# Another order of the products, output steps and side work of a convolution with a SwiGLU feed-forward

## The chip, the cores and the metric

The kernel runs on one core of a Trainium2 chip. The metric is the device time of one execution in microseconds (us). A measurement is the median of several executions; a profile is one more execution, taken by the hardware profiler. Engines are called by the profile's names: PE is TensorE (PEld its weight loads), DVE is VectorE, ACT is ScalarE, POOL is GpSimd, and SP is SyncE, whose queue issues nearly all DMAs (SPq).

## The reference

The input is x of 8 x 4096 tokens with 192 channels. A causal convolution over seven tokens with weights per head (eight heads of 24 channels, softmax over the seven taps) makes the tokens of a feed-forward network: RMS norm, two products with 192 x 1536 matrices, SiLU of one times the other, and a product with a 1536 x 192 matrix.

```python
w = np.exp(weight - weight.max(-1, keepdims=True)); w = w / (w.sum(-1, keepdims=True) + 1e-09)
out = np.einsum('hk,bskhg->bshg', w, x_unf)          # x_unf: 7 shifted copies of x, padded at the front
x = out.reshape(B * S, D)
xn = x / np.sqrt(np.mean(x * x, axis=-1, keepdims=True) + 1e-06) * rms_g
g = xn @ w_gate
val = xn @ w_val
return (g * (1.0 / (1.0 + np.exp(-g))) * val @ w_out).astype(np.float32)
```

## The kernel before

The 32768 tokens are cut into 32 *pairs* of 2 x 512 tokens (numbered 0 to 31). Pairs 0 and 1 run in their own way at the start, while the weights are converted and split into parts that go to DRAM (`wd`); pairs 2 to 31 are alike, and the change concerns them and the end of pair 1.

**Products of a pair (line 909).** The 1536 columns are handled in six groups j = 0 to 5, each with four cells a, b, c, d (two token halves times two column blocks). Each cell needs a gate and a value matrix product, which lie in the two halves of one *duo* of PSUM banks; there are four duos. A product is six matmuls, three parts of two, on 64 rows and 128 columns of the array. For j = 1 and 3 a cell is the sum of its products A, B, E. For j = 0, 2, 4, 5 a Strassen form with eleven products is used: P1, Q1, P2 go into a; P6, P7, Q3, P4 into b; P5, Q2, P3 into c; Q4 into d. Between them stand copies and sums in PSUM: f1 copies a to b (ACT, line 674) after P1 and before P6; f3 copies c to the scratch tile `tt` after P5 (ACT line 674, or DVE line 676); f4 makes c = b + tt (DVE, line 980) after P6 and before P7 and P3; f5 makes d = b + tt (line 980) after P7 and before P4, Q3 and Q4. So a.0, f4.5 and so on name a cell or an act and its group.

When a cell is complete, ga to gd take the SiLU (ACT, line 986) and ma to md multiply (DVE, line 993) into `ht`; both together give the duo back. A product that opens a cell (P1, P5, A) takes the duo that came free.

**Output steps (line 936).** Form and group, o1.0 to o7.5: 42 steps per pair, a Strassen form again, each of twelve matmuls on 128 rows and 32 columns of the array, into accumulators X, Z and Y, a duo each. The sums of halves h1 to h4 (DVE or POOL, line 963) prepare the operands of o5, o6, o7 and o3. After the o1 steps c1 copies X to Y; after o7, s7 copies Z, after o6, c2 copies X (ACT, line 674); at the end C22 and C21 add (DVE, line 1010), and the transposes T11, T12, T21, T22 (DVE, line 951) fill `o_sb`, from where st writes the output (line 1042) and which give X, Y, Z back.

**Work for later pairs.** ld loads rows of x (line 153) two pairs ahead; cv0 to cv6 are the taps of the convolution (ACT line 440, DVE line 444); sq, red, pow, bc, mul are the norm; pl stores the result to DRAM (line 1053); ft fetches it transposed (line 645) into `xb`. x1 to x4 are four sums of token halves (line 831); n, l, d split each of five operand groups 0 to 4 into three parts (n: ACT line 674; l: line 817; d: DVE line 819). Group 0 serves P1 and A, 1 serves P2, P4 and B, 2 the Q and E, 3 P5 and P6, 4 P7 and P3. The split weights come through a *ring* of ten slots; each use of a slot that is its last issues the next load (line 789). R, at the end of the first window, starts the ring.

**What sets the order.** Three strings written out by hand or by a planner. `LINE` is the order of products and steps in a pair. `ORDER` is one *window*: it interleaves the next n words of the line ("p4") with the acts; the first letter is the engine (V, A, G, S), a "+" means the next pair, a "-" the one before. It runs for windows 2 to 32. `FIRST` is window 1 (pair 1), in which W are pieces of the weight preparation. Every engine takes its instructions strictly in this order.

In before, the window begins with the last 15 steps of the pair before, then P1.0, and the 42 steps of a pair stand in one run.

Of the kernel before, what the change touches and what calls it, by code (L numbers as in the profile page):

```python
# [20 lines left out]
def kernel(  # L21
# [55 lines left out]
        "a5 b5 c5 d5",  # L77
    )
    ORDER = (
        "p4- Vd.3 Vl.3 Gh4.0- Gh4.2- p3- Vl.4 Vh4.1- Gl.1 Vd.4 Vh4.3- Vd.2 Vh4.5- Vcv1+ VC22-",  # L80
        "VT11- p8- Vcv2+ VT22- Vl.2 VC21- p1 Af1.0 VT12- VT21- p1 Af3.0 p1 Vcv3+ p1 Vf4.0 p2",
        "Vcv4+ p5 Agb.1 Vmb.1 Agc.0 Vf5.0 p1 Vmc.0 p1 Agd.0 Aga.0 p4 Sst0.0- Aga.1 Sst1.4-",
        "Sst0.1- Vcv5+ Vma.0 Vcv6+ Vma.1 Vmd.0 p1 Agb.0 p1 Asq+ p1 Vmb.0 Vred+ p1 Af1.2 p1",
        "Agc.3 Vmc.3 p4 Af3.2 Vf4.2 p2 Aga.2 Gpow+ p3 Vbc+ Vma.2 Vf5.2 Gmul+ p1 Spl.0+ Agc.2",
        "p2 Agd.3 Spl.1+ Sst1.2- Spl.2+ Agb.2 Vmc.2 Vmd.3 Spl.3+ Vmb.2 Vh1.0 Agd.2 p7 Agc.1",
        "Vmc.1 Vmd.2 Af1.4 p3 Agd.1 Vmd.1 Spl.4+ Spl.5+ Vf3.4 p2 Spl.6+ Vf4.4 Aga.4 Spl.7+ p2",
        "Vma.4 p2 Vf5.4 Agc.4 p3 Agb.3 Vmb.3 Vmc.4 p1 Agb.4 p2 Agd.4 Sft.0+ Sft.1+ Sft.2+",
        "Sst0.4- Vmb.4 Gh1.1 Gh1.2 Gh1.3 Sld.0++ Sft.3+ p1 Vmd.4 Af1.5 p1 Af3.5 Sld.1++",
        "Sld.2++ Sst1.0- p2 Aga.3 Vh3.2 Vf4.5 Vma.3 Sft.4+ Sld.3++ Sld.4++ Sld.5++ Sft.5+",
        "Sld.6++ Sst0.2- Sld.7++ Sst0.3- Sst1.1- Sst1.3- p3 Vf5.5 Aga.5 p4 Gh1.4 Gh3.1 Agc.5",  # L90
        "Gh3.4 p1 Vma.5 Gh3.0 Gh3.3 Vmc.5 An.0+ p1 Vx3+ Agd.5 Agb.5 Vl.0+ p5 Vmd.5 p2 Vmb.5",
        "Vh2.1 An.1+ Ac1 Vh1.5 Vx1+ p2 Gh2.0 Vh3.5 Vd.1+ Vx2+ Vh2.5 Vh2.2 Vh2.3 Vh2.4 p4",
        "Vh4.4 Vd.0+ Vx4+ p8 An.3+ An.4+ As7 Ac2 An.2+ Acv0++ p5",
    )
    FIRST = (
        "p1 Vcv5+ W p2 Vcv6+ p1 Aga.0 Vma.0 p2 Asq+ W W p1 Agb.0 W Vmb.0 W p1 Vred+ p2 Agc.0",
# [4 lines left out]
        "Vmc.2 p1 W p1 W W W p1 Agd.2 W p1 Vmd.2 W Vh1.2 p2 Vh3.2 Vh2.2 p1 Aga.3 W Vma.3 p1 W",  # L101
        "W W p1 W W p1 Agb.3 Sft.0+ Vmb.3 Sft.1+ p1 Sft.2+ p1 Sft.3+ W p1 Sft.4+ Agc.3 W W W",
        "Sft.5+ Vmc.3 p1 W W p2 Agd.3 p1 Vmd.3 Vh1.3 p1 W p1 W W Vh3.3 Vh2.3 W p1 Aga.4 W",
        "Vma.4 p3 Agb.4 W Vmb.4 p1 W p2 Agc.4 Vx3+ Vmc.4 p2 An.1+ p1 Agd.4 Vx1+ p1 Vmd.4",
        "Vd.1+ Vh1.4 p1 Vx2+ p1 Vh3.4 Vh2.4 Sld.0++ Vx4+ p1 Aga.5 Vma.5 An.3+ p2 An.2+ p1",
        "Agb.5 Vmb.5 p1 Sld.1++ p2 Gl.1+ Agc.5 Sld.2++ Vmc.5 p1 Vd.2+ p1 Vl.2+ Agd.5 p1 Vmd.5",
        "An.0+ Vl.0+ Vd.0+ An.4+ p1 Vh1.5 p1 Sld.3++ p1 Ac1 Sld.4++ Vh3.5 Vh2.5 p2 Sld.5++ p1",
        "Vh4.4 p1 Sld.6++ p1 R p2 Sld.7++ p6 As7 p1 Ac2 p4 Acv0++",
    )
    LINE = (  # L110
        "P1.0 P5.0 Ab.1 P6.0 Bb.1 Eb.1 P7.0 P3.0 Q2.0 P2.0 Q1.0 Q4.0 Aa.1 Ea.1 Ba.1 P4.0 Q3.0",
        "Ac.3 Ec.3 P1.2 Bc.3 P5.2 P6.2 Q1.2 P2.2 Ad.3 Ed.3 P7.2 Q2.2 P3.2 Bd.3 Q4.2 P4.2 Q3.2",
        "Ac.1 Ec.1 Bc.1 Ad.1 P1.4 Bd.1 Ed.1 P5.4 P6.4 Q1.4 Ab.3 P2.4 Eb.3 P7.4 Q2.4 P3.4 Bb.3",
        "Q3.4 P4.4 Q4.4 Aa.3 P1.5 Ea.3 P5.5 P6.5 Ba.3 Q1.5 P2.5 P7.5 Q2.5 P3.5 P4.5 Q3.5 Q4.5",
        "o1.0 o1.1 o7.0 o7.3 o1.2 o1.3 o1.5 o1.4 o7.2 o7.1 o2.4 o2.5 o6.0 o2.1 o6.3 o6.5 o2.2",
        "o7.5 o6.2 o6.4 o7.4 o6.1 o2.3 o4.0 o5.1 o5.5 o5.4 o5.0 o5.2 o5.3 o2.0 o4.5 o4.4 o4.3",
        "o3.1 o4.2 o4.1 o3.4 o3.3 o3.0 o3.5 o3.2",
    )

    cst = ctx.enter_context(tc.tile_pool(name="cst", bufs=1))  # L120
# [1176 lines left out]
```

## Time and profile before

| | |
|---|---|
| median of 3 executions | 2484.42 us (2483.5 to 2485.6) |
| profiled execution | 2486.79 us |
| its span | 2485.0 us |
| PE busy | 2464.4 us (99%) |
| DVE busy | 2051.4 us (83%) |
| ACT, POOL busy | 993.1 us (40%), 795.2 us (32%) |
| granted TensorE clock | 0.999 |

Busy time of an engine is the time in which one of its instructions runs; a matmul's end is modelled, so a waiting PE can be counted as busy, and starts of instructions tell more than busy shares. In the timelines a row is: start in us from the span's start, length, engine, line, operation, output <- inputs, shape, count, and in brackets the idle time before it with what ended it.

### The profile page before, as it was taken

What the parts mean: (1) busy time and instruction counts of PE and PEld (TensorE: products, weight loads), DVE (VectorE), ACT (ScalarE), POOL (GpSimd) and SP (SyncE); (2) the same over time, 40 slices, a digit from 0 to 9 for tenths busy, and PEclk for the clock granted to TensorE, in tenths of its full rate; (3) what the DMA queues carried; (4) which work ended last, traced back from release to release, by engine and by line L of the source; (5) the groups of instructions that cost most, each with busy time, mean ns of one, the idle gap of its engine ahead of it and who ended that gap; (6) DMA issues with size and microseconds to landing.
All of it is one profiled execution on the core that took longest, in us unless ns stands there. A gap on an engine that the chain in (4) does not pass through costs nothing.

```text
span 2485.0 us, 69316 instructions
## 1 busy us (share of the span) xinstructions
PE 2464.4 (99%) x29152; PEld 1923.9 (77%) x29152; DVE 2051.4 (83%) x2614; ACT 993.1 (40%) x1405; POOL 795.2 (32%) x566
## 2 busy tenths in 40 slices
PE   8999999999999999999999999999999999999998
PEld 5547778878787777788887778877788777888876
DVE  8688888888888888888888888888887888888864
ACT  6443334434344434344334343333344343444332
POOL 0541332323332323323323324233423233333222
PEclk9999999999999999999999999999999999999999
DMA  6364678666677666787667786666776666776653
GB/s 151 60 205 127 167 182 211 178 172 168 170 193 198 179 165 171 175 204 185 182 161 175 179 206 185 173 164 172 187 200 185 171 168 170 199 192 186 161 159 92
DMA packets 716392, 430.55 MB, mean 173 GB/s; under 512 B 510330, under 2 KB 702386, under 8 KB 716082
## 3 DMA queue, kind: packets, MB, share of 16 engines
q1 hardware_dynamic: 712336, 425.21, 66.6%
q8 instruction: 230, 3.77, 0.6%
q10 hardware_dynamic: 3746, 0.92, 0.2%
q14 instruction: 80, 0.66, 0.1%
HBM read 366.96 MB, written 58.98 MB: 171 GB/s over the span
## 4 chain that ended last, share of the span: by engine, by line
PE 94%; DVE 2%; DMA 1%; SPq 1%; issue 1%; POOL 0%; ACT 0%; DVEq 0%; POOLq 0%
PE ps L909 57%; PE ps L936 35%; PE ps L881 2%; DMA ht<-in_moe_w_gate_dram 0%; SPq L237 0%; DVE ht L1108 0%; DVE ht L963 0%; SPq L153 0%; DVE y L444 0%; DMA xb<-xd 0%; DMA x<-in_x_dram 0%; DMA hs<-in_moe_w_out_dram 0%; DVE part L344 0%; DMA ring<-wd 0%; POOL part L335 0%
## 5 line engine op out<-in xcount | busy, mean ns | idle before, releaser
L909 PE MATMUL ps<-part,ring 64*128 64x512 f32 x12240 | 1434.0, 390 | 2.6 <-DVE ps L980 0.4
L909 PEld LDWEIGHTS ps<-part,ring 64*128 64x128 f32 x12240 | 1174.3, 184 | 255.3 <-DVE ps L980 32.3
L986 ACT ACTIVATE tt<-ps 128x512 f32<-128x512 f32 x744 | 436.1, 599 | 714.4 <-PE ps L909 636.0
L993 DVE TENSOR_TENSOR ht<-ps,tt 128x512 f32<-128x512 f32 x744 | 495.5, 686 | 195.6 <-ACT tt L986 192.4
L936 PE MATMUL ps<-ht,wo_sb 128*32 128x384 f32 (+2 forms) x7272 | 471.6, 380 | 0.8 <-POOL wo_sb L336 0.8
L963 POOL TENSOR_TENSOR ht<-ht 128x512 f32<-128x512 f32 x182 | 279.0, 1563 | 568.7 <-PE ps L936 568.7
L936 PE MATMUL ps<-ht,x 128*32 128x256 f32 (+2 forms) x6696 | 429.1, 379 | 1.3 <-DVE ht L963 1.3
L936 PEld LDWEIGHTS ps<-ht,wo_sb 128*32 128x32 f32 x7272 | 332.4, 110 | 102.4 <-DVE tt L831 9.4
L980 DVE TENSOR_TENSOR ps<-ps,tt 128x1024 f32<-128x1024 f32 x240 | 295.6, 1232 | 97.8 <-ACT tt L674 55.6
L936 PEld LDWEIGHTS ps<-ht,x 128*32 128x32 f32 x6696 | 299.0, 110 | 87.5 <-DVE ht L963 2.0
L444 DVE SCALAR_TENSOR_TENSOR y<-xh,tp,y 128x1536 f32<-128x1536 f32 x186 | 338.9, 1822 | 2.5 <-ACT y L440 2.3
L674 ACT COPY ps<-ps 128x1024 f32<-128x1024 f32 (+1 forms) x151 | 134.0, 887 | 478.6 <-PE ps L909 367.9
L963 POOL TENSOR_TENSOR hs<-ht 128x512 f32<-128x512 f32 x120 | 165.5, 1390 | 405.2 <-DVE ht L993 405.2
L473 POOL TENSOR_SCALAR r<-r 128x8 f32<-128x8 f32 x31 | 6.1, 198 | 484.5 <-DVE r L468 484.4
L674 ACT COPY tt<-ps 128x1024 f32<-128x1024 f32 (+1 forms) x152 | 121.6, 800 | 68.7 <-PE ps L936 57.9
L963 DVE TENSOR_TENSOR ht<-ht 128x512 f32<-128x512 f32 x190 | 132.5, 698 | 9.7 <-PE ps L936 6.4
L936 PE MATMUL ps<-hs,x 128*32 128x128 f32 (+2 forms) x2232 | 130.1, 379 | 0.0
L936 PEld LDWEIGHTS ps<-hs,x 128*32 128x32 f32 x2232 | 94.0, 110 | 30.7
L674 ACT CAST part<-tt 128x1024 fp32r<-128x1024 f32 x60 | 62.9, 1049 | 136.8 <-DVE tt L831 136.8
L963 DVE TENSOR_TENSOR ht<-hs,ht 128x512 f32<-128x512 f32 x156 | 106.7, 729 | 1.2 <-PE ps L936 0.6
L819 DVE SCALAR_TENSOR_TENSOR part<-part,xb 128x1024 fp32r<-128x1024 f32 x87 | 105.9, 1218 | 0.0
L817 POOL TENSOR_TENSOR part<-xb,part 128x1024 fp32r<-128x1024 f32 x29 | 96.6, 3329 | 0.0
(131 smaller groups left out, 1436.5 us busy)
## 6 DMA issues: line engine op xcount, KB each, us to landing
ring<-wd SPq DMA_DIRECT2D x1440, 192.0 KB
xb<-xd SPq DMA_DIRECT2D x60, 512.0 KB
xd<-xh SPq DMA_DIRECT2D x240, 96.0 KB
xh<-in_x_dram SPq DMA_DIRECT2D x192, 105.0 KB
xb<-xd SPq DMA_DIRECT2D x60, 256.0 KB
out_dram<-o_sb SPq DMA_DIRECT2D x126, 96.0 KB
out_dram<-o_sb SPq DMA_DIRECT2D x62, 128.0 KB
wd<-part SPq DMA_DIRECT2D x5, 1152.0 KB
```

The costliest lines, as they stand in the source:

```text
L444: nc.vector.scalar_tensor_tensor(out=y, in0=xk, scalar=w, in1=y, op0=ALU.mult, op1=ALU.add)
L473: nc.gpsimd.tensor_scalar(out=r, in0=r, scalar1=s / D, scalar2=s * 1e-6, op0=ALU.mult, op1=ALU.add)
L674: nc.scalar.copy(out=dst, in_=src)
L817: e.tensor_tensor(out=split_of(g, 1).bitcast(F32R), in0=src, in1=high, op=ALU.subtract)
L819: nc.vector.scalar_tensor_tensor(out=split_of(g, 2).bitcast(F32R), in0=high, scalar=1.0 + SPLIT, in1=src, op0=ALU.mult, op1=ALU.subtract,)
L881: nc.tensor.matmul(out=self.both(j, c)[:, h, :], lhsT=wf[HALF[h], k, 2 * HOME[j] + f, :], rhs=rb[HALF[h], k, g, :], start=(k == 0), stop=( ...
L909: nc.tensor.matmul(out=self.both(j, c)[:, h, :], lhsT=left[HALF[h]], rhs=right[HALF[h]], start=(first and q == 0), stop=True, skip_group_c ...
L936: nc.tensor.matmul(out=self.acc(b)[i * Q : (i + 1) * Q, at : at + n], lhsT=left, rhs=cols, start=fresh, stop=True, skip_group_check=True, ...
L963: engine[eng].tensor_tensor(out=dst, in0=a, in1=b, op=op)
L980: nc.vector.tensor_tensor(out=self.both(j, c), in0=self.both(j, "b"), in1=s5, op=ALU.add)
L986: nc.scalar.activation(out=tt[:, t, :], in_=self.both(j, c)[:, 0, :], func=AF.Silu)
L993: nc.vector.tensor_tensor(out=self.hv(j, "abcd".index(c)), in0=self.both(j, c)[:, 1, :], in1=tt[:, t, :], op=ALU.mult,)
```

## The change

`ORDER`, `FIRST` and `LINE` are replaced by others; nothing else in the program changes. The multiset of products, steps and acts of a pair is the same, but:

- `LINE`: the 42 steps of a pair now stand in three places: five o1 steps after P7.5, then P4.5, Q3.5, Q4.5; then six steps; then the first product of the next pair, P1.0; then the other 31 steps. Inside the pair, groups are arranged anew: six products instead of three from P6.0 to P7.0, P3.5 ahead of P7.5, P5.4 ahead of P1.4.
- `ORDER`: a window begins with P1.0. With it, acts move over the window's edge: s7, c2, h2.4, h4.4 are done in the next window, and n.1 to n.4, d.1, x2 to x4 and cv0 stand at the head of the window of their pair.
- Engines: f3.4 moves from VectorE to ScalarE; x2, h1.0, h2.2, h3.2, h4.1 and l.4 from VectorE to GpSimd; h2.0, h3.1, h3.3, h4.0, h4.2 and l.1 from GpSimd to VectorE.
- `FIRST`: holds 83 words of pair 1's line instead of 99, so that pair 2's P1.0 comes ahead of 31 of pair 1's steps. All eight loads of pair 3's rows (Sld) stand behind R, where seven stood before it.

```diff
     ORDER = (
-        "p4- Vd.3 Vl.3 Gh4.0- Gh4.2- p3- Vl.4 Vh4.1- Gl.1 Vd.4 Vh4.3- Vd.2 Vh4.5- Vcv1+ VC22-",
-        "VT11- p8- Vcv2+ VT22- Vl.2 VC21- p1 Af1.0 VT12- VT21- p1 Af3.0 p1 Vcv3+ p1 Vf4.0 p2",
-        "Vcv4+ p5 Agb.1 Vmb.1 Agc.0 Vf5.0 p1 Vmc.0 p1 Agd.0 Aga.0 p4 Sst0.0- Aga.1 Sst1.4-",
...
+        "Gx2 p1 p6- An.3 An.1 p1- An.2 As7- Vh2.4- Vl.2 Vl.3 Vd.3 Vh4.0- p5- Ac2- Acv0+ p12-",
+        "Vx3 Vx4 Vd.1 Vd.2 Vl.1 p1- Vcv1+ Vh4.2- Vh4.3- Vh4.4- Vcv2+ VC22- Vh4.5- VT11- Vcv3+",
+        "VC21- Af1.0 An.4 p3- VT22- Gh4.1- Gl.4 p2- VT21- p1- VT12- p2 Af3.0 p5 Vd.4 Vf4.0",
+        "Vcv4+ Aga.0 Vma.0 p1 Agb.1 p2 Vmb.1 Vf5.0 p4 Vcv5+ p1 Agc.0 Vmc.0 p3 Aga.1 Agd.0",
+        "Agb.0 Vcv6+ Asq+ Vmd.0 p1 Vmb.0 Vma.1 Af1.2 p1 Vred+ p1 Agc.3 Af3.2 p3 Gpow+ Vmc.3",
...
+        "An.0+ p2 Gh1.4 Gh3.2 Gh3.4 Gh2.2 p2 Vh2.0 Vf5.5 Vmc.5 p3 Agb.5 Agd.5 Vd.0+ p1 Vx1+",
+        "Vl.0+ p2 Vmd.5 Vmb.5 Ac1 Vh2.1 Vh1.5 Vh2.3 Vh3.5 p3 Vh2.5",
     )
     FIRST = (
...
-        "An.0+ Vl.0+ Vd.0+ An.4+ p1 Vh1.5 p1 Sld.3++ p1 Ac1 Sld.4++ Vh3.5 Vh2.5 p2 Sld.5++ p1",
-        "Vh4.4 p1 Sld.6++ p1 R p2 Sld.7++ p6 As7 p1 Ac2 p4 Acv0++",
+        "Vd.2+ p1 Vl.1+ Agc.5 Vmc.5 p2 Agd.5 p1 Vmd.5 An.0+ Vd.0+ Vl.0+ p1 Ac1 Vh1.5 p2 Vh3.5",
+        "Vh2.5 p2 R Sld.0++ Sld.1++ Sld.2++ Sld.3++ Sld.4++ Sld.5++ Sld.6++ Sld.7++",
     )
     LINE = (
-        "P1.0 P5.0 Ab.1 P6.0 Bb.1 Eb.1 P7.0 P3.0 Q2.0 P2.0 Q1.0 Q4.0 Aa.1 Ea.1 Ba.1 P4.0 Q3.0",
...
-        "Q3.4 P4.4 Q4.4 Aa.3 P1.5 Ea.3 P5.5 P6.5 Ba.3 Q1.5 P2.5 P7.5 Q2.5 P3.5 P4.5 Q3.5 Q4.5",
+        "P1.0 P5.0 P6.0 Ab.1 P2.0 Eb.1 Q1.0 Bb.1 P7.0 Q2.0 P3.0 Aa.1 Ba.1 P4.0 Ea.1 Q4.0 Q3.0",
...
+        "P5.4 Ac.1 P1.4 Ec.1 Bc.1 P6.4 Q1.4 P2.4 Ad.1 Bd.1 Ed.1 Ab.3 Bb.3 P7.4 P3.4 Q2.4 Eb.3",
+        "P4.4 Q4.4 Q3.4 Aa.3 P1.5 Ea.3 P5.5 P6.5 Ba.3 Q1.5 P2.5 P3.5 Q2.5 P7.5 o1.0 o1.2 o1.4",
+        "o1.3 o1.5 P4.5 Q3.5 Q4.5 o7.0 o1.1 o7.1 o7.4 o7.3 o6.0 o6.1 o2.5 o6.5 o7.2 o2.0 o6.3",
...
     )
```

## The prediction

> **What bounds the kernel now.** I read the page first (its head, its busy times, its chain), then TensorE's timeline over one pair in the middle of the run, then the timeline of its weight loads over the same pair, and at last the start of the pipeline.
>
> The page of before:
>
> ```profile
> span 2485.0 us, 69316 instructions
> ...
> PE 2464.4 (99%) x29152; PEld 1923.9 (77%) x29152; DVE 2051.4 (83%) x2614; ACT 993.1 (40%) x1405; POOL 795.2 (32%) x566
> ...
> PE 94%; DVE 2%; DMA 1%; SPq 1%; issue 1%; POOL 0%; ACT 0%; DVEq 0%; POOLq 0%
> PE ps L909 57%; PE ps L936 35%; PE ps L881 2%; DMA ht<-in_moe_w_gate_dram 0%; SPq L237 0%; DVE ht L1108 0%; DVE ht L963 0%; SPq L153 0%; DVE y L444 0%; DMA xb<-xd 0%; DMA x<-in_x_dram 0%; DMA hs<-in_moe_w_out_dram 0%; DVE part L344 0%; DMA ring<-wd 0%; POOL part L335 0%
> ```
>
> TensorE is the chain: products (L909) and output steps (L936) are 92% of the span. But a stalled matmul counts as busy here, so waits must be read from starts. TensorE's timeline (start, length, engine, line, count), one pair:
>
> ```profile
> 1198.85 47.87 PE L909 MATMUL ps<-part,ring 64*128 64x512 f32 x408
> 1246.65 1.51 PE L936 MATMUL ps<-ht,wo_sb 128*32 128x384 f32 x24
> ...
> 1274.09 1.32 PE L909 MATMUL ps<-part,ring 64*128 64x512 f32 x8
> ```
>
> A pair takes 1274.09 - 1198.85 = 75.23 us: 68 products (408 matmuls) in 47.80, 42 steps in 27.44. Where nothing waits, products start 0.680 us apart (Q4.2 to P6.4, eighteen in a row), so 68 need 46.24. Steps start 0.645 to 0.650 apart; 42 x 0.650 = 27.30, and 0.137 is left at the end of the run. The product part is 47.80 - 46.24 = 1.56 too long. The weight loads of that part say where (in brackets: idle of the load path, and what ended it):
>
> ```profile
> 1198.85 0.53 PEld L909 LDWEIGHTS ps<-part,ring 64*128 64x128 f32 x6 [0.20 <-issue]
> 1199.67 3.30 PEld L909 LDWEIGHTS ps<-part,ring 64*128 64x128 f32 x30 [0.29 <-DVE o_sb L951]
> 1203.42 3.28 PEld L909 LDWEIGHTS ps<-part,ring 64*128 64x128 f32 x30 [0.45 <-DVE ps L980]
> 1207.14 24.42 PEld L909 LDWEIGHTS ps<-part,ring 64*128 64x128 f32 x216 [0.44 <-issue]
> 1231.79 7.36 PEld L909 LDWEIGHTS ps<-part,ring 64*128 64x128 f32 x66 [0.23 <-DVE ps L980]
> 1239.31 4.65 PEld L909 LDWEIGHTS ps<-part,ring 64*128 64x128 f32 x42 [0.15 <-ACT ps L674]
> 1244.35 1.93 PEld L909 LDWEIGHTS ps<-part,ring 64*128 64x128 f32 x18 [0.39 <-DVE ps L980]
> ```
>
> Normally a load runs 0.23 ahead of its matmul. Each bracket is a load that could not. By counts they are P5.0 (waits for the transpose T12), P7.0 (f4.0), Q4.0 (f5.0), P7.4 (f4.4), P6.5 (the copy f1.5), P4.5 (f5.5). From starts over 30 pairs, in medians, with the slow matmuls just behind: P5.0 0.20, P7.0 0.34, Q4.0 0.30, P7.4 0.11, P4.5 0.28, P6.5 0.05, and P6.2 0.07, whose load is late inside the long line. Together 1.35; the other 0.21 is the change of tiling, next. One law fits them: the cost is release + 0.13 us - due start (P6.2 released 0.06 early: 0.07; P7.4 0.02 early: 0.11; P7.0 0.19 late: 0.33).
>
> **Extra: four changes of tiling per pair.** Now each pair has one run of steps. After, it has three: five steps before P4.5, six before the next pair's P1.0, 31 behind it. Pair 1 already alternates, without waits at the joints:
>
> ```profile
> 182.82 0.86 PE L936 MATMUL ps<-ht,wo_sb 128*32 128x384 f32 x12
> 183.61 10.57 PE L881 MATMUL ps<-xb,part 64*128 64x512 f32 x48
> 194.11 1.51 PE L936 MATMUL ps<-ht,x 128*32 128x384 f32 x24
> ```
>
> A lone step takes 183.61 - 182.82 = 0.787, 0.137 over 0.650. The 48 matmuls between take 10.50 where 24 pairs of them at 0.429 need 10.30: 0.20 more. A round trip costs 0.337 there, and 0.347 by pair 15's own joints (0.106 into steps, 0.137 and 0.104 back). Two more round trips in each of 30 pairs: 60 x 0.347 = **+20.8 us**. These bounds are close; I take the row of the same kind of product.
>
> **Waits that go.** f4 starts 0.97 after its P6 starts (or f5 after P7), lasts 1.23 (group L980), and the load wants 0.05 + 0.13 more: 2.38 us, 3.5 products. P6.0 to P7.0: three products now (2.04: late by 0.34, as measured), six after (4.08). P7.5 to P4.5: three now; after, P7.5 and five steps, 0.79 + 3.25 + 0.14 = 4.17, while f5.5 stands behind ma.5 and h2.0 and ends near 3.7: margin 0.3. P7.0 to P4.0: f4.0 starts 1.25 behind P6.0, then cv4, ma.0, mb.1, f5.0 take 5.3 and the load 0.18, so 6.7; P4.0 is due eleven products, 7.5, behind P6.0. f4.4 loses f3.4 (1.21) from its front and gets nine products. T12's bank now goes to Ab.1, due 0.14 + 0.78 + 0.68 after the last step; T12 and its release need 1.1. So P5.0, P7.0, Q4.0, P7.4, P4.5 fall: 0.20 + 0.34 + 0.30 + 0.11 + 0.28 = 1.23.
>
> **Waits that stay or come.** P6.2 and P6.5 stay (0.12). P6.4 has only two products between P1.4 and itself, as P6.2 has: +0.07. VectorE's densest stretch is f4.0 to md.0: f4.0 1.15, cv4 to cv6 3 x 1.73, ma.0, mb.1, mc.0 3 x 0.60, f5.0 1.15, md.0 0.69, waits 0.22: 10.2, from 2.03 after P5.0's start. md.0 ends at 12.2, P1.2 takes its bank and is due after 18 products, 12.34: late by 0.04 with the release and lead. I take 0.07 (0 to 0.6, below). New: 0.14. Net per pair 1.23 - 0.14 = 1.09; the last pair has no successor's work and half the waits: 29.5 x 1.09 = **-32.1 us**.
>
> P1.0 ahead of 31 steps needs its bank from mb.5 (1.8 us earlier by VectorE's queue) and l.0 (3 us earlier). s7, c2, cv0, h2.4, h4.4, n.3, n.4 move across the window's edge; they keep their place among the steps, and ScalarE is idle for most of them (40% busy), so nothing for these. The fetch (sft) is issued about 6 us before n.0, as now; if n.0 is up to 2 us late, md.5's margin hides it. SyncE meets the stores, out-transfers and loads at later products; the ten ring slots cover ten products plus steps: nothing. VectorE and GpSimd swap six half-tile sums each way; neither sets the end at those places.
>
> **The start, once.** P1.0 of pair 2 now comes before 31 of pair 1's steps; at the first such place SyncE and ScalarE show
>
> ```profile
> 198.31 6.01 SPq L789 DMA_DIRECT2D ring<-wd  x10
> 204.36 0.56 SPq L153 DMA_DIRECT2D xh<-in_x_dram  x1
> 208.08 1.58 ACT L440 ACTIVATE y<-xh,tp 128x1536 f32<-128x1536 f32 x1 [2.19 <-DMA xh<-in_x_dram]
> ```
>
> The ring can only load when the last split has left its space (198.3); the packets of its first piece end near 200.1. P1.0 is due at 194.11 + 6 x 0.65 + 0.14 = 198.15: it waits **2.0**. Then all eight loads of pair 3's rows are queued behind R, where seven went before it. Seven took 6.9 us (181.5 to 188.4, by packets), so eight after the ring's packets (206.1) end at about 214; cv0 ends 1.6 later, then cv1, three h4, cv2 and C22 (5.7) are in order on VectorE, and o3.3, due at 217.3, starts at about 221.7: **4.4** more. Bounds: 0, if the transfers overlap better, to 9. Against it, o2.1 stalled 1.58 in the first window of before behind late rows: half of that, **-0.8**. At the end T21 no longer stands behind T12: **-0.5**.
>
> **Sum.** +20.8 - 32.1 + 2.0 + 4.4 - 0.8 - 0.5 = -6.2 us. The profiled execution took 2486.79 (span 2485.0 and 1.8 around it), 2.4 above the median 2484.42; so 2480.6 there, **2478.2** as median. About 0.2%, or 5 us (2479.4 and 2489.4), is what a measurement of this kernel tells from no change.
>
> **A rule against the change, weighed.** Row first: beside GpSimd's l.1, VectorE's l.2 takes 1.75 us instead of 1.22, and GpSimd's takes 3.37 instead of 2.36 at the start. After, l.4 is GpSimd's and d.4 VectorE's, at the same place. The Trainium skill, "SBUF — State Buffer", section "Who interferes with whom", says that a VectorE instruction with two SBUF inputs and a GpSimd one that reads SBUF exclude each other for the whole instruction. The trace agrees with that in both durations. By the rule the sum would be about +12 instead of -6, if d.4 comes second each time.
>
> **The rivals.** 1. *Slower: d.4 behind l.4.* n.4 follows f1.0 and ends near 19.2 us after P1.0; l.4 takes 2.36 alone (ends 21.6, before d.4 is due at 21.9) or, when it first meets cv3, 3.37 (22.5). Then f4.0 and all of the dense stretch is 0.6 late and P1.2 pays in full: 30 x 0.6 = 18, 2496. Against it: cv3 may come first and be over. It decides from 0.4 us of lateness on. Chance 0.16.
> 2. *The waits come back next door.* Ad.3, P5.2 and P3.5 have margins of 0.1 to 0.15 us only; 0.2 per pair returns: +6, 2484, no change. Chance 0.25.
> 3. *The start is hidden.* Ring and rows land in time: 2472. For it: transfers of 96-byte rows overlap in some windows. Chance 0.13.
> Forecast itself (2474 to 2483): 0.46, of which 0.36 lies below 2479.4.
>
> **Numbers.** Faster 0.36 + 0.13 + 0.02 of rival 2 = 0.51; slower 0.16 and 0.03 of rival 2's worst = 0.19; same 0.30. The range goes from 2469 (no start wait, no new waits) to 2493 (most of rival 1); leaving out its upper part and both tails costs about 0.2. The forecast's own range is 2474 to 2483.
>
> **What would show it.** In the profile after: a period near 74.85 us; three runs of L936 per pair of 5, 6 and 31 steps; no load of P7.0, Q4.0, P4.5 waiting on L980; P1.2 with at most 0.1; d.4 at 1.2 to 1.4 us; pair 2's P1.0 near 200.2 and a gap of 4 us before o3.3. Wrong, if the period stays above 75.1, if a lone P1.0 costs more than 0.35 beyond 0.68, or if d.4 takes 1.8.

## The result, and the profile after

The changed kernel takes 2481.32 us (median of 20 executions, 2479.56 to 2482.66); the kernel before, on the same chip, 2485.35 us (20 executions, 2483.5 to 2487.96). The ratio is 0.9983, 95% interval 0.9977 to 0.9990: 4.0 us less, or 0.17%. By the bound of 0.2% that is "no change", to which the prediction gave 0.30 (0.51 to "faster"); the time lies 3.1 us above the predicted 2478.2, inside the range. The profiled execution took 2480.53 us (before: 2486.79), so by the profiled pair the difference is 6.3 us; the sum below is made against that pair.

The page of the kernel after:

```profile
span 2478.7 us, 69365 instructions
...
PE 2456.4 (99%) x29152; PEld 1878.8 (76%) x29152; DVE 2015.3 (81%) x2585; ACT 1026.3 (41%) x1435; POOL 747.2 (30%) x565
...
PE 94%; DVE 2%; SPq 1%; DMA 1%; issue 1%; POOL 0%; ACT 0%; DVEq 0%; POOLq 0%; ACTq 0%
```

TensorE is the chain as before. TensorE's timeline shows a pair with its three runs of steps (start, length, engine, line, operation, tiles, shapes, count):

```profile
1246.62 3.46 PE L935 MATMUL ps<-ht,wo_sb 128*32 128x384 f32 x60
1250.01 2.37 PE L908 MATMUL ps<-part,ring 64*128 64x512 f32 x18
1252.30 0.86 PE L935 MATMUL ps<-ht,x 128*32 128x384 f32 x12
...
1256.34 0.97 PE L908 MATMUL ps<-part,ring 64*128 64x512 f32 x6
1257.24 0.86 PE L935 MATMUL ps<-ht,x 128*32 128x384 f32 x12
...
1277.52 43.96 PE L908 MATMUL ps<-part,ring 64*128 64x512 f32 x384
1321.41 3.46 PE L935 MATMUL ps<-ht,wo_sb 128*32 128x384 f32 x60
```

Five steps, three products, six steps, P1.0 alone, 31 steps, then 64 products. From the first step to the next first step: 1321.41 - 1246.62 = 74.79 us, where the kernel before took 75.23. Over all pairs, from P5.0 to the next P5.0, the median is 74.81 (29 pairs). The weight loads of the long product part show what is left of the seven late loads of before:

```profile
1277.52 25.76 PEld L908 LDWEIGHTS ps<-part,ring 64*128 64x128 f32 x228 [0.20 <-issue]
1303.44 12.81 PEld L908 LDWEIGHTS ps<-part,ring 64*128 64x128 f32 x114 [0.15 <-ACT ps L673]
1316.41 3.75 PEld L908 LDWEIGHTS ps<-part,ring 64*128 64x128 f32 x34 [0.15 <-ACT ps L673]
```

The first bracket is the change of tiling. The other two are the loads of P6.4 and P6.5, each behind the copy f1; the product itself is 0.025 us longer for it. No load waits for L979 (f4, f5) or for L950 (T12) any more.

The price was paid at the start of the pipeline. TensorE's timeline there, its waits (line, releaser: total, times, longest), and its windows (length, busy time of PE, PEld, DVE, ACT, POOL, then the granted clock, the DMA share and GB/s):

```profile
200.55 1.29 PE L908 MATMUL ps<-part,ring 64*128 64x512 f32 x6 [2.59 <-DMA ring<-wd]
201.77 1.51 PE L935 MATMUL ps<-ht,x 128*32 128x384 f32 x12
203.05 1.50 PE L935 MATMUL ps<-ht,wo_sb 128*32 128x384 f32 x12
...
224.57 5.79 PE L935 MATMUL ps<-ht,wo_sb 128*32 128x384 f32 x72 [5.07 <-DVE tt L1009]
```

```profile
PE ps L935 <- DVE tt L1009: 5.1, 1, 5.1
PE ps L908 <- DMA ring<-wd: 2.6, 1, 2.6
```

```profile
197.90:200.50 2.60, 0.06 (x4) 0.00 (x0) 2.46 (x4) 0.00 (x0) 0.00 (x0) 1.00 0.53 165
200.50:205.00 4.50, 4.45 (x42) 2.97 (x46) 2.39 (x3) 0.00 (x0) 0.00 (x0) 0.62 0.97 304
205.00:219.00 14.00, 14.00 (x266) 10.55 (x260) 2.06 (x2) 2.54 (x3) 0.05 (x1) 1.00 0.60 90
219.00:224.50 5.50, 0.50 (x12) 0.13 (x4) 5.50 (x7) 0.00 (x0) 1.56 (x1) 1.00 0.00 0
224.50:230.00 5.50, 5.43 (x70) 4.20 (x72) 4.40 (x10) 1.96 (x2) 2.18 (x1) 0.69 0.01 3
```

Both stalls that the prediction named are there: P1.0 of pair 2 stands for the ring's reload, o3.3 for C22 (L1009), which stands for the late rows. What it did not name is the clock column: behind each stall the granted clock is 0.62 and 0.69 for a stretch, and a step takes 1.28 us (201.77 to 203.05) where 0.645 is normal.

At the end, the timeline of VectorE and of the queues that issue the output DMAs:

```profile
2470.11 1.15 DVE L950 STREAM_TRANSPOSE o_sb<-tt 128x256 f32<-128x256 f32 x4
2471.10 4.97 ACTq L1041 DMA_DIRECT2D out_dram<-o_sb  x6
2471.29 3.72 SPq L1041 DMA_DIRECT2D out_dram<-o_sb  x4
2473.54 0.65 DVE L950 STREAM_TRANSPOSE o_sb<-ps 128x256 f32<-128x256 f32 x2 [2.28 <-PE ps L935]
```

T22 and T21 (the first row, 2470.11) are over before the last step ends; only T12 is left. In the kernel before, T12 and T21 both stood behind the last step, and so did all ten output DMAs:

```profile
2477.80 0.65 DVE L951 STREAM_TRANSPOSE o_sb<-ps 128x256 f32<-128x256 f32 x2 [2.69 <-PE ps L936]
2478.28 4.14 ACTq L1042 DMA_DIRECT2D out_dram<-o_sb  x6
2478.37 0.59 DVE L951 STREAM_TRANSPOSE o_sb<-tt 128x256 f32<-128x256 f32 x2
```

From the start of the last matmul to the end of the span it is 5.5 us, against 7.5 in the kernel before.

**Where the 6.3 us come from**, in the profiled pair: P5.0 of pair 2 starts at 230.28 us instead of 219.12 (+11.2); from there to P5.0 of pair 31 it is 2169.3 instead of 2184.5 (-15.2); the last pair -0.25; the end -2.0. Together -6.3.

### The profile page after: what moved, and what is told of

Same layout as the page of the kernel before. It is cut to its first block, busy times and chain, and to the rows that moved or that the text cites. A ratio compares the mean times of both kernels' runs of the same rounds, so it can differ in the third digit from the quotient of the medians.

```text
span 2478.7 us, 69365 instructions
## 1 busy us (share of the span) xinstructions
PE 2456.4 (99%) x29152; PEld 1878.8 (76%) x29152; DVE 2015.3 (81%) x2585; ACT 1026.3 (41%) x1435; POOL 747.2 (30%) x565
## 4 chain that ended last, share of the span: by engine, by line
PE 94%; DVE 2%; SPq 1%; DMA 1%; issue 1%; POOL 0%; ACT 0%; DVEq 0%; POOLq 0%; ACTq 0%
PE ps L908 57%; PE ps L935 35%; PE ps L880 2%; SPq L152 1%; DMA ht<-in_moe_w_val_dram 0%; SPq L236 0%; DVE y L443 0%; DVE ht L1107 0%; DVE ht L962 0%; DMA x<-in_x_dram 0%; DMA hs<-in_moe_w_out_dram 0%; DMA xh<-in_x_dram 0%; DVE part L343 0%; SPq L788 0%; POOL part L334 0%
## 5 line engine op out<-in xcount | busy, mean ns | idle before, releaser
L908 PEld LDWEIGHTS ps<-part,ring 64*128 64x128 f32 x12240 | 1134.2, 184 | 266.5 <-issue 11.9
L935 PE MATMUL ps<-ht,x 128*32 128x384 f32 (+2 forms) x6696 | 436.5, 381 | 0.0
L979 DVE TENSOR_TENSOR ps<-ps,tt 128x1024 f32<-128x1024 f32 x240 | 294.5, 1227 | 113.9 <-ACT tt L673 78.4
L443 DVE SCALAR_TENSOR_TENSOR y<-xh,tp,y 128x1536 f32<-128x1536 f32 x186 | 353.8, 1902 | 10.7 <-ACT y L439 10.6
L962 POOL TENSOR_TENSOR ht<-ht 128x512 f32<-128x512 f32 x121 | 169.3, 1409 | 606.8 <-DVE ht L962 489.9
L962 POOL TENSOR_TENSOR hs<-ht 128x512 f32<-128x512 f32 x150 | 191.5, 1295 | 416.4 <-DVE ht L992 416.4
L673 ACT COPY tt<-ps 128x384 f32<-128x384 f32 (+1 forms) x182 | 151.9, 835 | 274.2 <-PE ps L935 179.3
L962 DVE TENSOR_TENSOR ht<-ht 128x512 f32<-128x512 f32 x251 | 170.2, 697 | 13.1 <-PE ps L935 9.8
L935 PE MATMUL ps<-hs,x 128*32 128x128 f32 (+2 forms) x2232 | 145.3, 379 | 0.0
L816 DVE TENSOR_TENSOR part<-xb,part 128x1024 fp32r<-128x1024 f32 x87 | 105.7, 1215 | 0.3 <-ACT part L673 0.3
L493 POOL TENSOR_TENSOR xh<-y,s 128x1536 f32<-128x1536 f32 x30 | 89.7, 2990 | 12.0 <-DVE s L485 11.2
```

Source lines behind the costliest of these rows:

```text
L443: nc.vector.scalar_tensor_tensor(out=y, in0=xk, scalar=w, in1=y, op0=ALU.mult, op1=ALU.add)
L493: e.tensor_tensor(out=yn[p].rearrange("p a t -> p t a"), in0=y, in1=ss[:].rearrange("p (t o) -> p t o", o=1).to_broadcast([P, TB, GS]), op ...
L673: nc.scalar.copy(out=dst, in_=src)
L816: e.tensor_tensor(out=split_of(g, 1).bitcast(F32R), in0=src, in1=high, op=ALU.subtract)
L908: nc.tensor.matmul(out=self.both(j, c)[:, h, :], lhsT=left[HALF[h]], rhs=right[HALF[h]], start=(first and q == 0), stop=True, skip_group_c ...
L935: nc.tensor.matmul(out=self.acc(b)[i * Q : (i + 1) * Q, at : at + n], lhsT=left, rhs=cols, start=fresh, stop=True, skip_group_check=True, ...
```

## The experiments

All start from the changed kernel unless the text says otherwise. The "lateness" of a word of the line is the time from the start of the word ahead of it to its own start, less what that takes where nothing waits; where a word is late by less than 0.05 us, its own length is read instead, less 0.68.

**1. The rows earlier.** In `FIRST` only:

```diff
-... Vh3.4 Vl.2+ p1 Aga.5 ... p2 R Sld.0++ Sld.1++ ... Sld.7++
+... Vh3.4 Vl.2+ Sld.0++ Sld.1++ ... Sld.7++ p1 Aga.5 ... p2 R
```

> Only the first window is changed, on top of the changed kernel: the eight loads Sld of pair 2's rows stand ahead of Vx3+ (about 15 products earlier) instead of behind R at its end. Theory A (o3.3 of pair 2 waits for C, C for the tap cv0, cv0 for the rows, which left last on SP's queue): the 5.34 us gap ahead of o3.3 goes, and with it the 1.70 us that the following steps lost at half clock: 7.0 us less than the changed kernel, 2474.3 us. P1.0's wait for the ring, 2.66 us, and the 1.6 us of half clock behind it stay. Rival B (C is late because VectorE is, not because the rows are): no gain, 2481.3 us. Rival C (the half clock is not caused by the gap but comes with the place in the program): only the gap goes, 2476.0 us, and the granted clock behind o3.3 stays near 0.69.

(The rows are those of pair 3, as Sld++ in window 1 says.)

Measured: 2473.39 us, ratio to the kernel before 0.9958 (0.9945 to 0.9970). P5.0 of pair 2 starts at 223.29, 7.0 us sooner than in the changed kernel. Its windows at the same two places:

```profile
200.50:205.00 4.50, 4.50 (x46) 3.26 (x50) 2.35 (x3) 0.00 (x0) 0.00 (x0) 0.62 0.88 274
...
224.50:230.00 5.50, 5.50 (x50) 4.78 (x50) 5.26 (x6) 2.00 (x3) 0.00 (x0) 1.00 0.35 107
```

The gap ahead of o3.3 is gone and the clock behind it is 1.00; behind P1.0, whose wait of 2.6 us was left in place, it is 0.62 as before. So the rows were the cause of the second stall (not VectorE, rival B), and the slow clock comes with the stall (not with the place in the program, rival C).

**2. Both stalls away.** Experiment 1, and window 2 takes a list of its own; windows 3 to 32 keep `ORDER`:

```diff
-        run([w for row in ORDER for w in row.split()], w)
+        run([w for row in (SECOND if w == 2 else ORDER) for w in row.split()], w)
 # SECOND is ORDER with:
-"Gx2 p1 p6- ... VC21- Af1.0 An.4 ... p1- VT12- p2 Af3.0 ..."
+"Gx2 p6- ... VC21- An.4 ... p1- VT12- p1 Af1.0 p2 Af3.0 ..."
```

> The kernel of e1_rows_early, and in window 2 alone P1.0 stands behind the 31 steps, with its silu right behind it, as in the kernel before; all later windows are those of the changed kernel. Theory A (P1.0 waits for the ring's reload and the clock halves behind the gap): a further 2.66 + 1.6 us and one round trip of 0.35 us go, and up to 3.0 us of waits come in front of P1.0 and P5.0 (C and T12 of VectorE, late as in the kernel before), so 1.6 to 4.6 us less than e1: 2469.7 to 2472.7 us, taken 2472. Rival (the wait for the ring only moves to the next reader of the ring): no further gain, 2474.3 us.

Measured: 2470.70 us, ratio 0.9948 (0.9936 to 0.9961). No wait for the ring is left. The new waits at the products were smaller than feared: P6.0 starts 0.5 late behind the copy f1.0 and loses 0.1 more in its own matmuls. But o6.5, which the wait for the ring had covered, now waits for the half sum h2.5 (1.04 us late by starts):

```profile
199.60 1.51 PE L951 MATMUL ps<-ht,x 128*32 128x384 f32 x24 [0.81 <-DVE ht L978]
200.91 0.84 PE L951 MATMUL ps<-ht,wo_sb 128*32 128x384 f32 x12
```

Behind this shorter gap the steps run at their normal pace (0.65 us, granted clock 1.00). P5.0 of pair 2 starts at 219.41, as early as in the kernel before (219.12), and the pairs take 74.80 us. This is the best version of the study: about 13 us (0.5%) less than the kernel before, and some 9 us less than the changed kernel (0.9948 against 0.9983).

**3. One more split.** Q4.5 and its silu behind o7.0:

```diff
-"... P4.5 Q3.5 Q4.5 o7.0 o1.1 ..."
+"... P4.5 Q3.5 o7.0 Q4.5 o1.1 ..."
```

> The changed kernel with one product more split off: Q4.5 stands behind o7.0 instead of ahead of it, its add Agd.5 with it, so that there is one more round trip between the two tile shapes in each of the 30 pairs that repeat. Theory A (each round trip costs 0.347 us of TensorE's own time, and VectorE's banks are late by at most 0.2 us at P1.2 as a consequence): 10.4 to 17 us more than the changed kernel, 2492 to 2498 us; period 75.15 to 75.35 us. Rival (the change of shape is hidden by weight loads that run beside matmuls, and the split itself costs nothing): no change, 2481.3 us.

Measured: 2491.03 us, 1 us under the expected range, ratio 1.0028 (1.0016 to 1.0040), against 0.9983 for the changed kernel. The pair takes 75.15 us, 0.344 more; P1.2 is 0.033 us late (0.016 in the changed kernel), so the extra 0.2 that was allowed for it did not come. The price of a round trip between the two tile shapes is measured by itself: 0.34 us, not hidden by weight loads.

**4. The lock, brought about on purpose.** VectorE's d.4 beside GpSimd's l.4:

```diff
-"... VT22- Gh4.1- Gl.4 p2- VT21- p1- VT12- p2 Af3.0 p5 Vd.4 Vf4.0"
+"... VT22- Gh4.1- Gl.4 p2- Vd.4 VT21- p1- VT12- p2 Af3.0 p5 Vf4.0"
```

> The changed kernel with VectorE's Vd.4 moved ahead of VT21- (it stands behind Af3.0 in the list now), so that it falls beside l.4 on GpSimd. Theory A, the prediction's rival 1 brought about on purpose: VectorE's two-input operation and GpSimd's take turns, d.4 ends as late as l.4, T21 and T12 follow it, and Ab.1 waits about 1.9 us in every pair: period 76.6 us, 2535 to 2540 us. Rival (the two run beside each other at their own rates): no wait at Ab.1, period 74.8 us, 2481 us.

Measured: 2525.75 us (one execution), 9 us under the expected range; 76.42 us a pair. VectorE's and GpSimd's timelines at the same moment:

```profile
1068.74 2.40 DVE L818 SCALAR_TENSOR_TENSOR part<-part,tt 128x1024 fp32r<-128x1024 f32 x1
1071.06 0.63 DVE L950 STREAM_TRANSPOSE o_sb<-tt 128x256 f32<-128x256 f32 x2
```

```profile
1067.66 2.39 POOL L816 TENSOR_TENSOR part<-tt,part 128x1024 fp32r<-128x1024 f32 x1 [1.47 <-ACT part L673]
```

l.4 ends at 1070.05; d.4, begun at 1068.74, takes 2.40 us instead of 1.18: it stands until l.4 is over and then runs for 1.1. It does not read what l.4 writes. TensorE pays it through T12: the row of its waits is

```profile
PE ps L908 <- DVE o_sb L950: 37.5, 29, 1.4
```

and Ab.1 comes 1.49 us late by starts in the pairs 3 to 30 (1.9 was expected). The mechanism of rival 1 of the prediction is real; the order of the changed kernel avoids it for d.4.

**5. The title undone.** P1.0 behind the 31 steps in all windows:

```diff
-"Gx2 p1 p6- ... VC21- Af1.0 An.4 ... p1- VT12- p2 Af3.0 ..."
+"Gx2 p6- ... VC21- An.4 ... p1- VT12- p1 Af1.0 p2 Af3.0 ..."
```

> The changed kernel with its title undone in all windows: P1.0 stands behind the 31 steps, in front of P5.0, with its silu behind it; all else is as changed. Theory A (what P1.0 ahead of the steps buys is time for VectorE: C and T12 are done before the products read their banks): one round trip less, 0.35 us, but P1.0 waits 2.0 us for C and P5.0 1.0 us for T12; ledger 77.6 us a pair against 74.8, 2560 to 2565 us. Rival (the split is only overhead, VectorE is on time anyway): 74.45 us a pair, 2471 us. It is also a point on the clock: a wait of 2.0 us in every pair lies between the 1.5 us of e7_d4_early, behind which the steps ran at full clock, and the 2.5 us of e1_rows_early, behind which they ran at half; if it halves the clock too, the pair comes to 79 us or more.

Measured: 2585.71 us (one execution), 20 us above the expected range. P1.0 stands for C (1.82 us late by starts), P5.0 right behind it for T12 (0.7 us more), and the pairs are of two kinds: most of the fast ones take 77.30 us, close to the ledger, nearly all others 78.6 to 78.9. Windows behind P1.0's wait, of one pair of each kind:

```profile
2271.00:2275.00 4.00, 3.38 (x18) 2.55 (x18) 2.01 (x6) 2.01 (x2) 0.00 (x0) 0.57 0.27 73
...
2349.50:2353.50 4.00, 3.38 (x30) 2.50 (x28) 2.99 (x6) 2.01 (x2) 0.00 (x0) 1.00 0.36 108
```

In the first the clock is 0.57 and 18 matmuls start; in the second, 1.00 and 30. Of the pairs 3 to 30, 20 ran at half clock behind the wait and lost 1.3 to 1.6 us each (2.9 in one), 8 lost nothing, with the same two waits. The remaining excess is at the start, where o3.3 stood for 11.0 us. Even at full clock the split earns 2.5 us a pair (77.30 to 74.81), its own 0.35 already paid, by giving C and T12 time.

**6. The other split undone.**

```diff
-"... Q1.5 P2.5 P3.5 Q2.5 P7.5 o1.0 o1.2 o1.4 o1.3 o1.5 P4.5 Q3.5 Q4.5 o7.0 ..."
+"... Q1.5 P2.5 P7.5 Q2.5 P3.5 P4.5 Q3.5 Q4.5 o1.0 o1.2 o1.4 o1.3 o1.5 o7.0 ..."
```

> The changed kernel with the other split undone: P4.5 Q3.5 Q4.5 stand right behind P7.5 Q2.5 P3.5 and ahead of o1.0, with the operations that lead to them moved by as many products; P1.0 stays ahead of the steps. Theory A (the five steps between give GpSimd and VectorE the time for f5.5, and the round trip gives VectorE 0.35 us more a pair): one trip less, 0.35 us, against waits of 0.3 to 0.6 us each at P4.5, o6.5, P5.0, Ab.1, Aa.1 and P1.2; ledger 76.8 us a pair, 2536 to 2543 us. Rival (the split is overhead): 74.45 us a pair, 2471 us.

Measured: 2529.32 us (one execution), 7 us under the expected range; 76.51 us a pair, 1.70 more than in the changed kernel in spite of the trip saved. By starts, Aa.1 is 0.35 late, P1.2 0.21, o6.5 0.18, P5.0 0.14, P4.5 0.13 and Ab.1 0.11, most of them with 0.1 more in the matmuls just behind. These are the six places that were named beforehand, but all except Aa.1 lie below the 0.3 to 0.6 that had been expected there. The largest wait was not named: o6.0, 0.41 late, which stands for the copy c1 of ScalarE; o3.3 adds 0.08.

**7. f3.4 back on VectorE** (`Af3.4` becomes `Vf3.4` in `ORDER`).

> The changed kernel with the evacuation f3.4 back on VectorE, as the kernel before has it (ScalarE does it in the changed kernel). Theory A (nine words of TensorE lie between it and its reader, and VectorE has 0.3 us to spare there): no change, within 2 us of the changed kernel. Rival (VectorE is the engine that is late, so that each operation taken from it counts): up to 0.3 us a pair, 9 us more.

Measured: 2480.17 us, ratio 0.9982 (0.9972 to 0.9991), 74.79 us a pair: no change. The move of 1.2 us of work off an engine that is 81% busy bought nothing at this place.

**8. T21 last.** In window 32 alone `VT21-` stands behind `VT12-`.

> The changed kernel with T21 moved behind T12 in the last window alone, where the kernel before has it. Theory A (the end came 2.0 us sooner because T21 and its output DMAs were out of the way before the last step ended): 1.5 to 2.0 us more than the changed kernel, from the last matmul to the end 7.0 to 7.5 us instead of 5.5. Rival (the end is one landing time whichever DMA is last, and the 2 us came from elsewhere): 0 to 0.6 us.

Measured: 2482.56 us, ratio 0.9991 (0.9981 to 1.0000), 2.0 us above the changed kernel by the ratios, though the two intervals overlap, and 2.4 us above the kernel of experiment 7, timed beside it on the same chip. The timeline of the end bears it out:

```profile
2472.48 0.65 DVE L966 STREAM_TRANSPOSE o_sb<-ps 128x256 f32<-128x256 f32 x2 [2.80 <-PE ps L951]
2472.96 4.25 ACTq L1057 DMA_DIRECT2D out_dram<-o_sb  x6
2473.05 0.59 DVE L966 STREAM_TRANSPOSE o_sb<-tt 128x256 f32<-128x256 f32 x2
2473.15 2.06 SPq L1057 DMA_DIRECT2D out_dram<-o_sb  x4
```

All ten output DMAs are issued after T12 here, and from the last matmul to the end it is 7.6 us instead of 5.5.

**9. The title alone, on the kernel before.**

```diff
-"p4- Vd.3 Vl.3 Gh4.0- ... p8- Vcv2+ VT22- Vl.2 VC21- p1 Af1.0 VT12- VT21- p1 Af3.0 ..."
+"p1 p4- Vd.3 Vl.3 Gh4.0- ... p8- Vcv2+ VT22- Vl.2 VC21- Af1.0 VT12- VT21- p1 Af3.0 ..."
```

> The kernel before with the title alone: P1.0 at the head of the window, ahead of the last 15 steps of the pair before; its silu, the line and every other operation stay where the kernel before has them. Theory A (P1.0 ahead of the steps pays only together with a line that gives VectorE the time it thereby loses): one round trip more, 0.35 us; T12's bank goes to Ab.1 and its wait stays; f4.0 still follows f3.0 and T12 on VectorE while P7.0 comes one product sooner, so P7.0 waits 0.7 us instead of 0.35; ledger 0.70 us a pair more than the kernel before, 75.9 us, 30 x 0.7 = 21 us, and 0 to 4 us for the ring at pair 2: ratio to the kernel before 1.0085 to 1.010, 2504 to 2509 us. Rival (the title is the gain: the first product hides the wait for T12): 0.2 us a pair less, ratio 0.9975, 2478 us.

Measured: 2503.02 us, 1 us under the expected range, ratio 1.0069 (1.0052 to 1.0086); 75.86 us a pair, 0.62 more than the kernel before. The trip is 0.35 of it; the rest is mostly P7.0, 0.51 late by starts where 0.19 had been (0.7 had been expected), because VectorE's f4.0 has one product less ahead of its reader. P1.0 did not wait for the ring, since it stands ahead of 15 steps here, not 31. So the title costs 17 us by itself and earns its price only in the rearranged line.

## Why the prediction was right, and where it was wrong

**The pairs: right.** Net 1.09 - 0.69 = 0.396 us a pair was forecast, 0.43 came (75.23 to 74.81). Of its parts, two more round trips at 0.347: experiment 3 measured 0.344 for one. A lone P1.0 takes 0.897 us to the next step; with the longer steps ahead of it and behind it (0.788 and 0.669 where 0.645 is normal) that is 0.38 more than without the joints, a little over the 0.35 that the prediction set as a bound. Waits that stay: 0.26 forecast at P6.2, P6.5, P6.4 and P1.2, about 0.16 measured, and P1.2 (the densest stretch of VectorE) at 0.016 instead of 0.07. The five waits that were to fall have fallen. Experiments 5, 6 and 9 show why both belong together: the trips buy VectorE time, and undone one at a time they cost 1.7 us a pair or more.

**The start: the failed step.** Forecast 2.0 + 4.4 = 6.4 us; measured 11.2 to P5.0 of pair 2, of which 0.35 is the trip, so 10.8. The two waits were 2.66 and 5.34, inside their bounds; the landing time of the rows varies (the gap ahead of o3.3 was 4.5 to 6.1 in the runs that left this place alone, experiments 3, 7 and 8). The term that was missing is the clock behind the waits: P1.0 and the steps behind it lost 1.6 us, o3.3 and its followers 1.7, together 3.3. Waits and slow clock make 11.3; the stretch is entered 0.26 us sooner than in the kernel before, and the 0.2 us that P5.0 waited there are gone. The prediction put the slow clock at nothing: it does not name it. Experiment 1 removed the one stall and its slow stretch and left the other; experiment 2 removed both.

**The stalls of before: under-priced.** -0.8 was put for rare stalls of the kernel before. Its 29 intervals from P5.0 to P5.0 add up to 2184.5, and 29 x 75.233 = 2181.8: 2.7 us of such stalls, 1.7 of them in its first interval. There o6.3 (the prediction names o2.1, the word ahead of it) starts 1.58 us late, waiting for a half sum of VectorE (L963). VectorE had waited 1.14 us for the fetched `xb` (DMA xb<-xd) a few operations earlier; that late rows were behind it, as the prediction says, is not shown. These stalls are gone in the windows after.

**The end: under-priced.** -0.5 forecast, -2.0 measured. The prediction named only the transpose; what moved were its output DMAs, which had stood in the queues together with those of T12 (experiment 8).

**The sum.** -6.2 forecast, -6.3 in the profiled pair: the match is luck, for the errors cancel. Without its trip, which belongs to the pairs, the start is 10.8 us (+4.4 on the forecast); the pairs are 29 x -0.427 - 0.25 + 0.35 = -12.3 (forecast 20.8 - 32.1 = -11.3, so -1.0), the stalls -1.9 and the end -1.5 off. By medians it is 4.0 us, because the profiled execution of before lies 1.4 us above its median and that of after 0.8 below. The case "faster by over 0.2%" was missed by 0.03%; without the start's stalls it would have been right.

**The rivals.** Rival 1 (d.4 behind l.4) did not happen: d.4 takes 1.18 us in the changed kernel, 1.42 at most. The reason given was close: it is cv3 that meets GpSimd (the h4.1 ahead of l.4), 2.37 us instead of 1.81, and there VectorE has time. Experiment 4 shows what the rule from the Trainium skill ("SBUF — State Buffer", "Who interferes with whom") costs where it bites: 1.6 us a pair. Rival 2 (the waits come back next door) is refuted by the loads above, and rival 3 (a hidden start) by the waits; its 2472 is about what experiments 1 and 2 reached (2473.4 and 2470.7) by making the start so.

## What to carry to other kernels

A split of a run of equal matmuls has a fixed price (0.34 us a round trip here), and what it buys is time for the engine that feeds the banks: count both in the same place, and do not judge the split without the line that goes with it. Look at the one-time start of a pipeline as closely as at its period: this reordering won 12 us over 29 pairs and gave back 11 in the first, of which moving eight DMA issues returned 7. And when TensorE waits for 1.8 us or more within a few microseconds, price the slow clock that can follow, mostly 1.3 to 1.9 us here, and not the length of the wait alone.

## What the runs showed of the hardware

TensorE's granted clock can halve behind a wait. By lateness from starts:

| wait | where | behind it |
|---|---|---|
| 1.0 us | o6.5, experiments 2 and 5 | full clock |
| 1.5 us | Ab.1, experiment 4, 28 pairs | full clock |
| 1.6 us | o6.3 of pair 2, kernel before | full clock |
| 1.8 us, and 0.7 us more behind one product | P1.0 and P5.0, experiment 5, 28 pairs | half clock in 20, 1.3 to 1.6 us lost in all but one |
| 2.5 us and more | P1.0 of pair 2 and o3.3 of pair 1, changed kernel and experiments 1, 3, 4, 6, 7 and 8 | half clock each time, mostly 1.5 to 1.9 us lost, 2.3 and 2.9 in two places |

The records of the granted clock in the traces show what decides. In each of the eleven traces all changes of the clock lie on a grid of 3.413 us, within 0.005 us, and a slow stretch behind a wait is one, two or three steps of that grid long (3.41, 6.83 or 10.24 us). Here is the window of the grid that holds P1.0's wait, and the one behind it, in a slow pair of experiment 5, then in a fast one (columns as above):

```profile
462.20:465.61 3.41, 1.50 (x10) 0.97 (x12) 3.41 (x9) 1.00 (x1) 0.00 (x0) 1.00 0.05 9
465.61:469.02 3.41, 3.41 (x18) 2.67 (x18) 1.84 (x3) 1.01 (x1) 0.00 (x0) 0.50 0.50 136
383.69:387.10 3.41, 1.68 (x24) 0.79 (x14) 3.41 (x6) 0.00 (x0) 0.36 (x1) 1.00 0.00 0
387.10:390.51 3.41, 2.79 (x26) 2.27 (x26) 2.41 (x5) 2.01 (x2) 0.00 (x0) 1.00 0.38 106
```

In the slow pair both waits fall into one window: TensorE stands idle for 1.91 of its 3.41 us, and the next window has half the clock. In the fast pair the same two waits are cut by the edge of the grid, 1.73 and 0.62 us, and the clock stays. Counted over all windows at full clock in the eleven traces, with idle time as the profile gives it (the ends of matmuls are modelled): up to 1.74 us idle, the next window was always at full clock; above 2.0 us it was always at half; between the two, 12 times at half and twice at full. So about half a window of idle time is enough, in one wait or in two, and the same wait costs nothing when the edge of a window cuts it. The waits of experiment 4 fill at most 1.33 us of a window by this count.

The Trainium skill, "TensorE: Matmul & The Clock Gate", section "Part 1: The HAM clock gate (the "warmup" mystery)", says that the gate looks at activity in a free-running window of 3413 ns, goes to half after an idle window and back after a busy one. The grid agrees with the free-running window and its length. Most losses agree with one window at half clock (1.3 to 1.9 us where half of 3.41 is 1.7). That a whole idle window is needed is not what the runs show: 1.75 to 2.0 us of it were enough in most cases.
